# Two weight matrices cast to bf16 by the DMA that loads them, in place of f32 loads and eight cast instructions

## The chip, the core and the metric

The kernel runs on one core of one Trainium2 chip. The core has five engines with queues of their own: TensorE (PE, matmuls), VectorE (DVE), ScalarE (ACT), GpSimd (POOL) and SyncE (SP), which here issues the DMAs. Each engine takes its instructions in program order. Sixteen DMA engines move the data. The metric is the device time of one execution in microseconds (us). Five runs of the kernel before gave a median of 202.45 us (201.94 to 202.56).

## The reference

First a gated linear attention over 4 batches of 8 heads, 768 steps and head size 48: a state of 48 x 48 is scaled row by row with alpha and takes up an outer product at each step, and the output is q times the state. The heads side by side are 3072 tokens of width 384. They go through a feed-forward layer with the gate h cos(h).

```python
for t in range(S):
    state = alpha[:, :, t, :, None] * state + np.einsum('bhd,bhe->bhde', k[:, :, t], v[:, :, t])
    y[:, :, t] = np.einsum('bhd,bhde->bhe', q[:, :, t], state)
...
h = x @ w_in          # w_in  384 x 2048, f32
g = h * np.cos(h)
return (g @ w_out)    # w_out 2048 x 384, f32
```

All inputs and the output are f32; the kernel's matmuls work on bf16.

## The kernel before

The tokens are cut into 24 chunks of 128 steps, 6 per batch. For each chunk j the kernel runs a row of units, each with a letter in the dictionary `units` (lines 380 to 402); the order of all units is written out by hand in two strings, START for the first chunks and STEPS for the rest, and `run` calls them one by one. This order is the order in every engine's queue. A unit is written as its letter and a number, as in "T2": transposes of chunk 2.

The units of the attention: `a`, `k`, `v` load alpha, k and q, and v (192 KB each, in runs of 48 f32); `l` or `i` take the logarithm of alpha on ACT (L148); `C` or `c` sum it up with matmuls (L161, L165); `E` or `d` take the exponentials on ACT (L179, L181). `o` and `O` scale k and q into the tile kqb and cast v into vpb, and prepare a decay Em: in `o` all on POOL, in `O` with q on DVE (L191 to L197). `T` transposes kqb on PE (L210) and `t` copies the result out of PSUM on DVE (L216). `A` are the scores (L233), `m` masks them on DVE (L242). `S` is the state's increment (L255), `u` adds it on DVE (L267) and scales it, on POOL for most chunks (L269). `Y` are the outputs (L310), `y` copies them out on DVE (L315). The results of T, S and Y share one PSUM buffer, tagged "g".

The units of the feed-forward layer: `F` and `G` are the two halves of the first product (L329) with w1, over the first and the last 8 of 16 blocks of w_in's columns; `f` and `g` are its cosines on ACT (L337); `p` and `q` the gates on DVE (L344). `V`/`X` and `W` are the two halves of the second product (L353) with w2; `x` and `e` take the result out of PSUM, and `e` stores it. The results of C, A, F and G share three PSUM buffers, tagged "big". `w20` is 20 matmuls on a tile of zeros (L376), which fill PE's queue: 47 of them stand before c0, the first sum of logarithms, and 32 more among the units that follow.

The weights come in four loads of 1536 KB: `z0` and `z1`, the two halves of w_in's columns (in rows of 4 KB), and `Z0` and `Z1`, the two halves of w_out's rows (in rows of 1.5 KB). SP issues them into the f32 tiles w1f and w2f (L114, L128). Each half is then cast to bf16 in two pieces, one on DVE (L121; units `1` and `3`) and one on ACT (L119; units `2` and `4`): 10 and 20, 11 and 21, 30 and 40, 31 and 41.

Of the kernel before, what the change touches and what calls it, by code (L numbers as in the profile page):

```python
# [9 lines left out]
FP = mybir.dt.float32  # L10
BF = mybir.dt.bfloat16
AF = mybir.ActivationFunctionType
# [4 lines left out]
def kernel(  # L17
# [10 lines left out]
    nc = tc.nc  # L28
    B, H, S, D = q.shape
    DM, DF = moe_w_in.shape  # L30
    C = 128
# [3 lines left out]
    NF = DF // C  # L35
# [9 lines left out]
    consts = ctx.enter_context(tc.tile_pool(name="consts", bufs=1))  # L45
# [34 lines left out]
    m2 = consts.tile([C, 2], FP, tag="m2")  # L80
# [1 line left out]
    nc.vector.memset(m2[0:64, 0:1], 1.0)  # L82
    nc.vector.memset(m2[64:128, 1:2], 1.0)

    w1f = consts.tile([C, 3, DF], FP, tag="w1f")
    w1 = consts.tile([C, 3, DF], BF, tag="w1")
    w2f = consts.tile([C, NF, DM], FP, tag="w2f")
    w2 = consts.tile([C, NF, DM], BF, tag="w2")

    a_t, q_t, k_t, v_t, cp_t, icp_t = {}, {}, {}, {}, {}, {}  # L90
# [20 lines left out]
        v_t[j] = t  # L111

    def load_w1(f0, f1):
        nc.sync.dma_start(out=w1f[:, :, f0:f1],  # L114
                          in_=moe_w_in[:, f0:f1].rearrange("(k p) f -> p k f", p=C))

    def cast(eng, dst, src):
        if eng is nc.scalar:
            eng.activation(out=dst, in_=src, func=AF.Copy)  # L119
        else:  # L120
            eng.tensor_copy(out=dst, in_=src)  # L121

    def cast_w1(half, eng, k0, k1):
        f = slice(half * (DF // 2), (half + 1) * (DF // 2))
        cast(eng, w1[:, k0:k1, f], w1f[:, k0:k1, f])

    def load_w2(f):
        nc.sync.dma_start(  # L128
            out=w2f[:, f : f + 8],
            in_=moe_w_out[f * C : (f + 8) * C, :].rearrange("(f p) n -> p f n", p=C),  # L130
        )

    def cast_w2(eng, f0, f1):
        cast(eng, w2[:, f0:f1], w2f[:, f0:f1])


    table = [None]

# [234 lines left out]
    def warmup(n):  # L373
# [5 lines left out]
    dve, act_e, pool = nc.vector, nc.scalar, nc.gpsimd  # L379
# [14 lines left out]
        "i": lambda j: ln(j, 1), "c": lambda j: cums(j, 1), "d": lambda j: exps(j, 1),  # L394
        "w": warmup,

        "1": lambda h: cast_w1(h, dve, 0, 2), "2": lambda h: cast_w1(h, act_e, 2, 3),
        "3": lambda h: cast_w2(dve, 8 * h, 8 * h + 5), "4": lambda h: cast_w2(act_e, 8 * h + 5, 8 * h + 8),

        "a": load_a, "k": load_qk, "v": load_v,  # L400
        "z": lambda h: load_w1(h * (DF // 2), (h + 1) * (DF // 2)), "Z": lambda h: load_w2(8 * h),
    }

    def run(order):
# [3 lines left out]
                units[u[0]](n)  # L408

    START = (  # L410
# [6 lines left out]
    )  # L417
# [38 lines left out]
```

## Time and profile before

| | us |
|---|---|
| median of 5 runs | 202.45 |
| the profiled execution, its own time | 202.56 |
| its span | 200.8 |
| PE busy in the span | 191.1 |
| DVE / ACT / POOL busy | 126.3 / 126.5 / 78.9 |
| weight loads issued by SP at | 9.74, 21.12, 22.16, 25.49 |
| a half of w1, issue to landing | 7.6 and 8.4 |
| a half of w2, issue to landing | 11.7 and 14.0 |
| casts on DVE start at | 17.62, 30.31, 36.13, 43.02 |
| casts on ACT start at | 19.88, 29.94, 36.75, 43.44 |

A line of a timeline gives start, length, engine, line of the code, operation, output and inputs, and in brackets the idle time before it with what ended it. The chain of waits is the chain of work that ended last, followed back from the last instruction. The profiler names the tiles w1 and w2 "w", and many others "t"; lines that differ only in the buffer are told apart by their place in the hand-written order.

### The profile page before, as it was taken

Reading aid. Unit: us, or ns where it says so; the run is one execution under the profiler, and the core shown is the slowest. Engines: PE = TensorE matmul, PEld = TensorE weight load, DVE = VectorE, ACT = ScalarE, POOL = GpSimd, SP = SyncE. Lnnn points to the kernel's source line nnn. Section 1 sums busy time; section 2 is a strip of 40 time slices with the busy share of each in tenths; the row PEclk is TensorE's granted clock in tenths of the full one; section 3 lists DMA queues with packets and bytes.
Section 4 is the critical chain, followed back from the end, with each engine's and each line's share of the span. In section 5 each row is a group of like instructions: output and inputs, shape, how many; then the busy total and the mean of one; then the engine's idle time right before and its main releaser. Section 6 shows DMA issues by size and latency. Waiting matters only on the chain.

```text
span 200.8 us, 5940 instructions
## 1 busy us (share of the span) xinstructions
PE 191.1 (95%) x2535; PEld 141.1 (70%) x2535; DVE 126.3 (63%) x146; ACT 126.5 (63%) x139; POOL 78.9 (39%) x124
## 2 busy tenths in 40 slices
PE   7998979999899999999999999999999999999981
PEld 2443558597677878878877878788778778787750
DVE  6207577986966775676658656756767486658220
ACT  2024858889699379588496694795785955343510
POOL 3005190255558621923818208419471167011000
PEclk9999999999999999999999999999999999999999
DMA  6999999999898699889899799995999897100111
GB/s 121 192 285 254 218 367 340 274 173 199 167 239 170 148 183 172 173 159 185 198 188 197 160 189 163 212 194 149 205 147 131 135 185 147 42 32 12 39 58 63
DMA packets 123098, 34.47 MB, mean 172 GB/s; under 512 B 117184, under 2 KB 122304, under 8 KB 123072
## 3 DMA queue, kind: packets, MB, share of 16 engines
q1 hardware_dynamic: 123072, 34.09, 87.0%
q8 instruction: 20, 0.33, 0.7%
q14 instruction: 6, 0.05, 0.1%
HBM read 25.17 MB, written 4.72 MB: 149 GB/s over the span
## 4 chain that ended last, share of the span: by engine, by line
PE 82%; DVE 7%; issue 5%; DMA 2%; SPq 1%; POOL 1%; ACT 0%; POOLq 0%; DVEq 0%; ACTq 0%
PE t L329 31%; PE o_new L353 31%; PE t L310 7%; PE t L233 3%; DMA t<-in_k_dram 2%; DVE g_new L344 2%; PE t L210 2%; PE cum_new L161 2%; PE w_ps L376 2%; PE t L255 2%; DVE t L242 1%; DVE t L216 1%; DVE t L315 1%; SPq L105 1%; PE cum_new L165 1%
## 5 line engine op out<-in xcount | busy, mean ns | idle before, releaser
L337 ACT ACTIVATE c_sb<-t,halfpi 128x1024 bf16<-128x1024 f32 x48 | 53.4, 1115 | 33.6 <-PE t L329 33.3
L329 PE MATMUL t<-t,w 128*128 128x128 bf16 x1152 | 72.0, 219 | 1.0 <-DVE t L315 0.7
L329 PEld LDWEIGHTS <-w 128*128 128x128 bf16 x1152 | 67.0, 98 | 6.2 <-DVE t L315 0.8
L353 PE MATMUL o_new<-w,g_new 128*128 128x384 bf16 x384 | 69.9, 326 | 0.7 <-ACT o_sb L369 0.6
L344 DVE TENSOR_TENSOR g_new<-t,c_sb 128x1024 bf16<-128x1024 f32 x48 | 58.3, 1217 | 7.0 <-ACT c_sb L337 6.6
L353 PEld LDWEIGHTS <-g_new 128*128 128x128 bf16 x384 | 34.7, 98 | 22.6 <-issue 1.2
L242 DVE TENSOR_TENSOR t<-t,mask_f 128x1024 bf16<-128x1024 f32 x24 | 29.3, 1223 | 32.3 <-PE t L233 32.3
L269 POOL TENSOR_TENSOR ub<-sc,Em 128x384 bf16<-128x384 f32 x20 | 16.6, 829 | 61.9 <-DVE sc L267 61.9
L191 POOL TENSOR_TENSOR kqb<-t,icp_new 128x384 bf16<-128x384 f32 x24 | 24.8, 1034 | 27.2 <-ACT icp_new L179 19.4
L193 POOL TENSOR_TENSOR kqb<-t,cp_new 128x384 bf16<-128x384 f32 x22 | 21.9, 998 | 1.0 <-DMA t<-in_q_dram 0.9
L376 PE MATMUL w_ps<-warm 128*128 128x512 bf16 x79 | 20.9, 414 | 1.3 <-DVE warm L58 1.2
L369 ACT ACTIVATE o_sb<-o_new 128x384 f32<-128x384 f32 x22 | 10.9, 493 | 17.8 <-PE o_new L353 17.8
L315 DVE CAST t<-t 128x384 bf16<-128x384 f32 x24 | 13.4, 556 | 10.0 <-PE t L310 10.0
L195 POOL CAST vpb<-t 128x384 bf16<-128x384 f32 x24 | 12.4, 517 | 13.7 <-DMA t<-in_v_dram 12.0
L179 ACT ACTIVATE icp_new<-cum_new 128x768 f32<-128x768 f32 (+1 forms) x13 | 9.9, 762 | 9.8 <-PE cum_new L165 9.8
L141 ACT ACT_TABLE_LOAD x12 | 15.4, 1283 | 0.9 <-PEq L440 0.7
L310 PE MATMUL t<-t,vpb 128*64 128x128 bf16 x288 | 15.6, 220 | 0.4 <-DVE sc L267 0.3
L376 PEld LDWEIGHTS <-warm 128*128 128x128 bf16 x79 | 7.8, 105 | 11.2 <-issue 3.7
L148 ACT ACTIVATE lnab<-a_new 128x768 bf16<-128x768 f32 (+1 forms) x13 | 10.2, 798 | 8.5 <-DMA a_new<-in_alpha_dram 8.5
L337 ACT ACT_TABLE_LOAD x12 | 15.4, 1283 | 0.2
L310 PE MATMUL t<-t,ub 128*64 128x128 bf16 x160 | 12.9, 225 | 0.9 <-DVE t L216 0.8
L310 PEld LDWEIGHTS <-ub 128*64 128x64 bf16 x160 | 9.8, 109 | 5.4 <-issue 2.9
(43 smaller groups left out, 124.8 us busy)
## 6 DMA issues: line engine op xcount, KB each, us to landing
t<-in_v_dram SPq DMA_DIRECT2D x24, 192.0 KB, 3.9
a_new<-in_alpha_dram SPq DMA_DIRECT2D x24, 192.0 KB, 4.6
t<-in_k_dram SPq DMA_DIRECT2D x24, 192.0 KB, 4.4
t<-in_q_dram SPq DMA_DIRECT2D x24, 192.0 KB, 4.6
out_dram<-o_sb SPq DMA_DIRECT2D x24, 192.0 KB, 2.4
w1f<-in_moe_w_in_dram SPq DMA_DIRECT2D x2, 1536.0 KB, 8.0
w2f<-in_moe_w_out_dram SPq DMA_DIRECT2D x2, 1536.0 KB, 12.9
t<-kqb SPq DMA_TRANSPOSE x16, 4.3
```

Of the source, the lines that this page charges most:

```text
L141: nc.scalar.preload_act_table_set("natural_log_exp_and_others")
L191: nc.gpsimd.tensor_tensor(out=kqb[:, j % 3, 0, :, 0:D], in0=k_sb, in1=icp.rearrange("s (h d) -> s h d", h=H), op=ALU.mult)
L193: qeng.tensor_tensor(out=kqb[:, j % 3, 1, :, 0:D], in0=q_sb, in1=cp[:, 0:HD].rearrange("s (h d) -> s h d", h=H), op=ALU.mult)
L242: nc.vector.tensor_tensor(out=t.rearrange("s (h t) -> s h t", h=H), in0=A_ps.pop(j).rearrange("s (h t) -> s h t", h=H), in1=mask_f.unsquee ...
L269: eng.tensor_tensor(out=ub[:, j % 3, :, 0:96].rearrange("r p (a e) -> r p a e", a=2), in0=sc.rearrange("r p (a e) -> r p a e", a=2), in1=E ...
L310: nc.tensor.matmul(t[64 * half : 64 * half + 64, kt * C : (kt + 1) * C], lhsT, rhs, start=start, stop=stop, skip_group_check=True)
L315: nc.vector.tensor_copy(out=t.rearrange("r k t -> r (k t)"), in_=y_ps.pop(j)[:, 0 : 3 * C])
L329: nc.tensor.matmul(t[:, f], w1[:, kk, ft * C : (ft + 1) * C], x_t[j][:, kk], start=(kk == 0), stop=(kk == 2))
L337: nc.scalar.activation(out=c_sb, in_=h_ps[j, half], func=AF.Sin, bias=halfpi, scale=1.0)
L344: nc.vector.tensor_tensor(out=g_t[j][:, half * HF : (half + 1) * HF], in0=h_ps.pop((j, half)), in1=c_t.pop((j, half)), op=ALU.mult)
L353: nc.tensor.matmul(o_ps[j][:, 0:DM], g_t[j][:, ft], w2[:, ft], start=(f == 0 and (half == 0 or not whole)), stop=(f == HF - 1 and (half == ...
L376: nc.tensor.matmul(w_ps, warm[:, 0:C], warm, start=True, stop=True)
```

## The change

The f32 tiles and the eight cast instructions go. The four weight loads write bf16 straight into w1 and w2, and are issued by POOL in place of SP. In START they are placed earlier: z0 right after the first two logarithms, ahead of the warm-up matmuls; z1 after O0; Z0 after O1; Z1 after o2. On POOL's own queue z0 therefore follows the last of its constant tiles, z1 stands between O0 and O1, Z0 between O1 and u1, and Z1 between o2 and o3.

```diff
-    w1f = consts.tile([C, 3, DF], FP, tag="w1f")
     w1 = consts.tile([C, 3, DF], BF, tag="w1")
-    w2f = consts.tile([C, NF, DM], FP, tag="w2f")
     w2 = consts.tile([C, NF, DM], BF, tag="w2")
...
     def load_w1(f0, f1):
-        nc.sync.dma_start(out=w1f[:, :, f0:f1],
+        nc.gpsimd.dma_start(out=w1[:, :, f0:f1],
                           in_=moe_w_in[:, f0:f1].rearrange("(k p) f -> p k f", p=C))
-    def cast(eng, dst, src):
...
-    def cast_w1(half, eng, k0, k1):
...
     def load_w2(f):
-        nc.sync.dma_start(
-            out=w2f[:, f : f + 8],
+        nc.gpsimd.dma_start(
+            out=w2[:, f : f + 8],
             in_=moe_w_out[f * C : (f + 8) * C, :].rearrange("(f p) n -> p f n", p=C),
         )
-    def cast_w2(eng, f0, f1):
...
-        "1": lambda h: cast_w1(h, dve, 0, 2), "2": lambda h: cast_w1(h, act_e, 2, 3),
-        "3": lambda h: cast_w2(dve, 8 * h, 8 * h + 5), "4": lambda h: cast_w2(act_e, 8 * h + 5, 8 * h + 8),
...
     START = (
-        "v0 a0 k2 k0 a1 i1 a2 a4 a3 i0 w20 w20 w7 c0 d0 O0 w7 T0 z0 t0 S0 k1 10 c1 d1 l1 u0 v1 "
-        "w8 C1 O1 A0 m0 v2 w5 T1 t1 20 w6 S1 u1 A1 a5 Y0 y0 E1 o2 F0 k3 z1 Z0 v3 m1 l2 Z1 f0 v5 "
-        "T2 t2 p0 a8 Y1 y1 k4 v4 o3 a9 11 w3 S2 u2 A2 m2 N0 a6 21 F1 G0 T3 t3 f1 G1 g0 a7 Y2 k5 "
-        "p1 g1 30 C2 40 q0 y2 w3 X1 q1 A3 m3 a10 E2 S3 k6 F2 x1 f2 u3 v7 Y3 41 y3 31 G2 G3 g3 "
+        "v0 a0 k2 k0 a1 i1 a2 a4 a3 i0 z0 w20 w20 w7 c0 d0 O0 z1 w7 T0 t0 S0 k1 c1 d1 l1 u0 v1 "
+        "w8 C1 O1 Z0 A0 m0 v2 w5 T1 t1 w6 S1 u1 A1 a5 Y0 y0 E1 o2 Z1 F0 k3 v3 m1 l2 f0 v5 "
+        "T2 t2 p0 a8 Y1 y1 k4 v4 o3 a9 w3 S2 u2 A2 m2 N0 a6 F1 G0 T3 t3 f1 G1 g0 a7 Y2 k5 "
+        "p1 g1 C2 q0 y2 w3 X1 q1 A3 m3 a10 E2 S3 k6 F2 x1 f2 u3 v7 Y3 y3 G2 G3 g3 "
         "p2 k7 o4 q3 a11 X0 F3 g2 q2 T4 x0 v6 o5 W0 t4 f3 l4 A4 S4 e0 u4 N2 m4 W1 l3 p3 Y4 y4 "
```

More of the change, by code (lines that the diff above doesn't have):

```diff
@@ L113, in load_w1 @@
     def load_w1(f0, f1):
-        nc.sync.dma_start(out=w1f[:, :, f0:f1],
+        nc.gpsimd.dma_start(out=w1[:, :, f0:f1],
                           in_=moe_w_in[:, f0:f1].rearrange("(k p) f -> p k f", p=C))
-    def cast(eng, dst, src):
[L118 to L121, printed above, removed]
-    def cast_w1(half, eng, k0, k1):
-        f = slice(half * (DF // 2), (half + 1) * (DF // 2))
-        cast(eng, w1[:, k0:k1, f], w1f[:, k0:k1, f])
     def load_w2(f):
-        nc.sync.dma_start(
-            out=w2f[:, f : f + 8],
+        nc.gpsimd.dma_start(
+            out=w2[:, f : f + 8],
             in_=moe_w_out[f * C : (f + 8) * C, :].rearrange("(f p) n -> p f n", p=C),
         )
-    def cast_w2(eng, f0, f1):
-        cast(eng, w2[:, f0:f1], w2f[:, f0:f1])
     table = [None]
```

## The prediction

> **What bounds the kernel now.** I read first the busy table and the slices of the page, then the windows by stage, then the chain of waits in order of time, and last the timelines of the engines that the change touches.
>
> ```profile
> PE 191.1 (95%) x2535; PEld 141.1 (70%) x2535; DVE 126.3 (63%) x146; ACT 126.5 (63%) x139; POOL 78.9 (39%) x124
> ...
> DMA  6999999999898699889899799995999897100111
> ```
> ```profile
> 20.00:30.00 10.00, 8.24 (x117) 5.77 (x115) 6.43 (x9) 6.93 (x8) 5.79 (x9) 1.00 1.14 290
> ...
> 80.00:100.00 20.00, 20.00 (x304) 16.00 (x302) 13.47 (x15) 12.93 (x15) 12.36 (x19) 1.00 0.95 179
> ```
>
> In the windows the columns after the length are busy PE, PEld, DVE, ACT and POOL, then granted clock, DMA share and GB/s. From 60 us on PE is busy 20.00 of 20.00 us at clock 1.00: nothing that the change touches lives there, so the second 140 us pass unchanged and the start is passed on whole. All eight casts lie before 45 us. The second thing to see is the DMA row: the 16 DMA engines are full from 2 us on, so whatever is loaded earlier makes something else later.
>
> The chain of waits in the only place where a cast is on it:
>
> ```profile
> 35.13 1.00 issue
> 36.13 0.79 DVE w L121
> 36.91 0.39 issue
> 37.30 1.21 DVE g_new L344
> 38.51 0.47 DVE t L315
> 38.98 0.86 DVE g_new L344
> 40.03 1.21 DVE t L242
> 41.24 0.47 DVE sc L267
> 41.75 0.75 PE t L310 x20
> ```
>
> DVE runs gate p1 in the first "issue" (from 35.00), then cast 30 (L121), and from there it sets the pace up to Y3 at 41.75.
>
> The front of the kernel, from the timelines of ACT, PE and POOL:
>
> ```profile
> 10.21 0.94 ACT L148 ACTIVATE lnab<-a_new 128x384 bf16<-128x384 f32 x2 [8.19 <-DMA a_new<-in_alpha_dram]
> ```
> ```profile
> 14.10 0.33 PE L161 MATMUL cum_new<-lnab,triu_bf 128*128 128x384 bf16 x1
> ...
> 27.31 0.76 PE L210 MATMUL t<-ident_bf,kqb 128*128 128x128 bf16 x8
> ```
> ```profile
> 20.47 0.50 POOL L195 CAST vpb<-t 128x384 bf16<-128x384 f32 x1 [0.52 <-DMA t<-in_v_dram]
> 20.93 0.20 POOL L197 TENSOR_TENSOR Em<-cp_new,m 128x8 f32<-128x8 f32 x1
> 24.87 0.83 POOL L269 TENSOR_TENSOR ub<-sc,Em 128x384 bf16<-128x384 f32 x1 [3.74 <-DVE sc L267]
> 25.66 1.00 POOL L191 TENSOR_TENSOR kqb<-t,icp_new 128x384 bf16<-128x384 f32 x1
> 26.62 0.99 POOL L193 TENSOR_TENSOR kqb<-t,cp_new 128x384 bf16<-128x384 f32 x1
> ```
>
> The logarithms wait for alpha tile 1 (landing 10.21) and end at 11.15. The matmul c0 that reads them starts only at 14.10, when the 47 warm-up matmuls queued before it are over: alpha has 2.95 us of slack. T2 on PE (from 27.31) needs kqb of chunk 2, ready on POOL at 26.62 + 0.99 = 27.61: no slack at all.
>
> **The change part by part.** The sum is made against the profiled execution: span 200.8, time 202.56, 1.76 around the span, which I keep; it is 0.11 above the median of 202.45, so I add the difference to the median. A measurement of this kernel tells no less than about 0.2% (0.4 us) from no change.
>
> *Casts removed.* Four on DVE (1.22, 1.22, 1.25, 1.15) and four on ACT (1.06, 1.06, 1.16, 1.15). Those of w1 are hidden: the first DVE one (17.62) ends before its queue next waits for q (0.17 us on DMA), the second (30.31) is followed by a state and a mask whose readers run at 35.6, and ACT waits for PE after both of its own. The last two, 43.02 and 43.44, are followed by waits for PE or ACT (DVE 1.18 at 46.47, ACT 0.73 at 45.33). Only cast 30 at 36.13 is on the chain. Without it gate q0 runs 36.13 to 37.30, y2 and q1 end near 38.9; then m3 needs the scores A3 (PE 39.10 to 39.43, behind X1, which starts after fillers at 37.66 anyway), so m3 starts at 39.45 instead of 40.03. F2, which waited 0.38 for q1, starts at 39.77. The next late thing is A3: the gain is not 1.13 but 40.03 - 39.45 = **-0.6 us**, and PE carries it on through G2, G3, X0, F3, W0 without a gap. Bounds 0 and -1.1.
>
> *First load of w1 moved to the start, on POOL's queue.* It was issued by SP at 9.74, behind all ten first loads; now POOL issues it after its last mask instruction at 2.03 + 0.29 = 2.3, with no wait. Its 1536 KB moved at about 410 GB/s while alone (13.6 to 17.6 us), that is 3.84 us of all 16 engines. The engines are full with the 192-byte runs of q, k, v and alpha, so if the whole half goes first, alpha 1 lands at 10.21 + 3.84 = 14.05, the two logarithms end at 15.0 and c0 starts 0.9 late: **+0.9 us**, straight into the chain, since the later fillers are a fixed count. Lower bound 0: if the cast load costs by the bytes that it writes, 1.92 us, it fits in the slack of 2.95. Upper bound: at the 187 GB/s that the 192-byte runs get, 8.4 us, which is 5.4 past the slack. I take the rate of the same bytes in 4 KB rows, the nearest row. F0 at 25.96 has its weights in all these cases.
>
> The page DMA: Bandwidth & Descriptors of the Trainium skill, section Queues, rings and completion order, says that each DMA engine turns round-robin between queue rows, packet by packet; no stretch of this trace has two data queues, so it is not shown here. By it the weights would not wait behind the ten loads, as on one queue, but cut in among them. The same page's fit for loads issued by GpSimd (section Anatomy of one DMA, about 2.0 us plus bytes at 436 GB/s) gives 5.6 us for this half, an estimate; landed by 8, all of it would be ahead of alpha 1.
>
> *The other three loads on POOL.* Each issue now stands between compute on POOL. No POOL row shows such an issue; SP took 1.00 for a half of w1, and 0.49 and 4.62 for a half of w2 (the latter held up by a full queue), about 0.5 to 1.1 for the many 192 KB loads with the same 1,024 runs. I take 1.1 and keep 0.49 and 4.62 as ends.
> z1, behind O0 (end 17.05), has 1.9 us before O1 starts at 18.95, and T1 (22.06) leaves 2 us more: hidden up to 3.9.
> Z0 stands behind O1, whose v cast waits for v1, and in front of u1 (24.87) and o2, which have no slack. v1's landing, 20.47 before, has the same bytes ahead of it plus z1 if that goes first: between 20.5 and 24.3. I take the late end, as for alpha. Then the v cast and Em end at 25.0, Z0's issue at 26.1, where u1 would want 24.74 + 0.9 = 25.64: T2 is late by **+0.5 us**, and with it t2, the gate p0 behind it on DVE, and Y1, which shares the PSUM buffer. Bounds 0 (v1 early) and 25.0 + 4.62 - 25.64 = 4.0.
> Z1 behind o2 delays o3 (end 30.14), which T3 wants at 33.9: hidden up to 3.7. Landings: z1 is wanted by G0 at about 32.5, Z0 by X1 at 37.7, Z1 by W0 at 48.2; with 8.4 us, the slower landing of a half of w1, they come by about 27, 35 and 38: hidden.
>
> *SP's queue* loses four issues (7.1 us together) and runs its loads earlier; after 8 us no load is on the chain, so this is worth nothing.
>
> The sum: -0.6 + 0.9 + 0.5 = +0.8 us, 202.45 + 0.8 = **203.25**.
>
> A rule against the change, in SBUF — State Buffer of the skill (section A bandwidth-pool intuition that's wrong): DVE copies of f32 within SBUF lock GpSimd out while it writes descriptors. The DVE casts that would do so (128x2048 in 1.22 us) are the ones that leave, so by it the sum stays; no run shows it.
>
> **The rivals.**
> 1. *Everything is hidden* (the other side: faster). The place is c0, the price 0.9. If alpha 1 lands before 13.15, the point from which c0 is not delayed, and v1 early, only -0.6 is left: 201.85. For it: 2.95 us of slack, and half the bytes written. Against: DMA share 1.05 to 1.45 from 2 to 12 us, no free engine. Chance 0.22.
> 2. *Only the front is paid*: v1 comes early or the issue is short, +0.9 - 0.6 = +0.3: 202.75, no difference. Chance 0.15.
> 3. *POOL is held by its issues.* At SP's longest, 4.62, o2 is 4.0 late: -0.6 + 0.9 + 4.0 = +4.3, 206.75. For it: 1,024 runs per half of w2, and POOL idle for only 3.74 before u1. Against: SP's 4.62 was a full queue. Chance 0.15.
> 4. *The casting transfer is slow*, 8.4 us a half: c0 5.4 late, -0.6 + 5.4 = +4.8, 207.25, and more if v1 waits for a second such half (8.4 + 4.6 on 20.4 is 33.4, where S1 would want 23.8 + 5.4 = 29.2: +4.2, 211.4). For it: no cast load is in this trace. Against: nothing but the plain load's 410 GB/s. Chance 0.15.
> The forecast itself, +0.4 to +2, has 0.33.
>
> **How the numbers follow.** Slower 0.33 + 0.15 + 0.15 = 0.63, same 0.15, faster 0.22. The range reaches from the hidden case, with 0.1 for scatter, 201.75, to the case of long issues, 206.8; outside are most of rival 4 and the far ends of the others, under 2 in 10. The forecast's own range is 202.85 to 204.5.
>
> **What would show it.** Right: the logarithms start near 14 instead of 10.21, c0 near 15.0; on POOL u1 follows the issue of Z0 without idle time and T2 waits for kqb; no cast between p1 and q0, and m3 waits for A3; from 60 us on PE is full and only shifted. Wrong: c0 still at 14.10 (hidden), c0 near 19.5 (slow cast), a gap of several us on POOL before u1 (long issue), or a wait of F0, G0 or X1 for a weight, which I hold to be covered. The code could also spend time on POOL before its first issue; the sooner alpha then lands, the smaller the front term.

## The result, and the profile after

The changed kernel took a median of 203.76 us (29 runs, 202.89 to 208.08) against 202.54 us for the kernel before (53 runs, 201.61 to 204.13). The ratio is 1.0059, with a 95% interval of 1.0044 to 1.0074: slower by about 1.2 us. Medians and ranges, here and below, are of all runs; the ratios leave out runs that lie more than 1.5% above the fastest of their kernel, three of these 29. The profiled execution took 203.63 us with a span of 201.9; before it was 202.56 with 200.8. So 1.1 us of span are to be found.

The page of the changed kernel, its busy times, its DMA row, the queue that POOL feeds, and its weight loads:

```profile
PE 191.0 (95%) x2535; PEld 141.1 (70%) x2535; DVE 122.4 (61%) x142; ACT 122.5 (61%) x135; POOL 81.5 (40%) x128
...
DMA  6999999999999389889999699988994996201112
...
q0 software_dynamic: 2880, 3.15, 9.4%
...
w<-in_moe_w_in_dram POOLq DMA_DIRECT2D x2, 768.0 KB, 8.8
w<-in_moe_w_out_dram POOLq DMA_DIRECT2D x2, 768.0 KB, 10.1
```

DVE and ACT each lost four instructions and about 4 us of work, and the span grew: the work that went was not what set the end. The four loads now have a queue of their own (q0), which before did not exist, and deliver 768 KB of bf16 each, in 8.8 us (w1) and 10.1 us (w2), medians of two loads. The windows by stage, with the same columns as before the change:

```profile
20.00:30.00 10.00, 8.39 (x100) 5.57 (x99) 5.90 (x8) 5.24 (x8) 6.57 (x10) 1.00 1.20 198
80.00:100.00 20.00, 20.00 (x297) 15.78 (x295) 13.41 (x15) 13.65 (x16) 11.37 (x17) 1.00 1.03 167
```

As before, PE is full from 60 us on; every matmul there comes a constant 1.74 us later than before (57.62 became 59.36, 185.53 became 187.28). The whole difference at PE is made in the first 45 us. The chain of waits in that stretch of the changed kernel:

```profile
20.13 7.41 DMA t<-in_q_dram
...
27.61 0.84 ACT lnab L132
28.46 0.02 issue
28.48 1.28 ACT L321
29.76 0.01 issue
29.77 1.12 ACT c_sb L321
30.89 0.02 issue
30.92 1.22 DVE g_new L328
32.14 0.48 DVE t L299
32.62 0.05 issue
32.66 0.34 PE t L239 x4
...
43.50 0.75 PE t L294 x20
```

Two things are new. Cast 30 between two gates is gone from it. And a DMA stands on it at 20 us: the logarithm of unit l2, then the table load for the cosine, the cosine f0, gate p0, the copy y1 and S2 (32.66) follow one another with no gap. The profile puts the wait down to a load of q; the logarithm reads alpha of chunks 4 and 5, and it is the alpha load of chunk 5 (a5) that came last, as this answer on the DMA issues from 18.0 to 18.8 us of the changed kernel shows (KB each, then us to landing):

```profile
w<-in_moe_w_in_dram POOLq DMA_DIRECT2D x1, 768.0 KB, 9.0
a_new<-in_alpha_dram SPq DMA_DIRECT2D x1, 192.0 KB, 9.5
```

a5 was issued at 17.98 and landed at 27.5. Before, it was issued at 17.95, took 4.6 us, and l2 ran at 22.63:

```profile
22.63 0.84 ACT L148 ACTIVATE lnab<-a_new 128x768 bf16<-128x768 f32 x1 [0.29 <-DMA a_new<-in_alpha_dram]
```

S2 on the chain of the kernel before:

```profile
30.45 0.34 PE t L255 x4
```

The front, on ACT's timeline of the changed kernel:

```profile
14.48 0.94 ACT L132 ACTIVATE lnab<-a_new 128x384 bf16<-128x384 f32 x2 [12.47 <-DMA a_new<-in_alpha_dram]
...
27.61 0.84 ACT L132 ACTIVATE lnab<-a_new 128x768 bf16<-128x768 f32 x1 [3.98 <-DMA t<-in_q_dram]
```

The logarithms began at 14.48 in place of 10.21, and the matmul c0 at 15.47 in place of 14.10, with 1.15 us of idle time ahead of it that ACT ends:

```profile
15.47 0.32 PE L145 MATMUL cum_new<-lnab,triu_bf 128*128 128x384 bf16 x1 [1.15 <-ACT lnab L132]
```

POOL around the issue of Z0 (the middle line):

```profile
18.37 0.81 POOL L112 DMA_DIRECT2D w<-in_moe_w_in_dram  x1
...
22.23 0.94 POOL L116 DMA_DIRECT2D w<-in_moe_w_out_dram  x1
...
26.26 0.82 POOL L253 TENSOR_TENSOR ub<-sc,Em 128x384 bf16<-128x384 f32 x1 [3.09 <-DVE sc L251]
```

POOL stands idle for 3.09 us after that issue and u1 waits for DVE, not for POOL.

The 1.1 us are this sum of the two profiled executions (us; the first row is the first exponential on ACT, which follows c0; a positive difference is later):

| stretch | before | after | difference |
|---|---|---|---|
| start to first exponential | 14.54 | 15.91 | +1.37 |
| first exponential to S2 | 15.91 | 16.75 | +0.84 |
| S2 to Y3 | 11.30 | 10.84 | -0.46 |
| Y3 to the start of ACT's last eviction | 155.09 | 155.08 | 0 |
| that start to the end of the span | 3.96 | 3.32 | -0.64 |
| span | 200.8 | 201.9 | +1.1 |

### The profile page after: what moved, and what is told of

It reads as the page before. It is cut to its first block, busy times and chain, and to the rows that moved or that the text cites. A ratio compares the mean times of both kernels' runs of the same rounds, so it can differ in the third digit from the quotient of the medians.

```text
span 201.9 us, 5935 instructions
## 1 busy us (share of the span) xinstructions
PE 191.0 (95%) x2535; PEld 141.1 (70%) x2535; DVE 122.4 (61%) x142; ACT 122.5 (61%) x135; POOL 81.5 (40%) x128
## 4 chain that ended last, share of the span: by engine, by line
PE 79%; SPq 9%; DMA 4%; DVE 3%; ACT 2%; issue 1%; ACTq 0%; DVEq 0%
PE o_new L337 32%; PE t L313 31%; PE t L294 7%; SPq L103 6%; DMA t<-in_q_dram 4%; PE t L217 3%; SPq L98 3%; PE cum_new L145 2%; PE t L239 2%; PE t L194 1%; DVE g_new L328 1%; SPq L108 1%; DVE t L226 1%; PE cum_new L149 1%; ACT L321 1%
## 5 line engine op out<-in xcount | busy, mean ns | idle before, releaser
L175 POOL TENSOR_TENSOR kqb<-t,icp_new 128x384 bf16<-128x384 f32 x24 | 23.9, 998 | 26.3 <-ACT icp_new L163 20.2
## 6 DMA issues: line engine op xcount, KB each, us to landing
w<-in_moe_w_out_dram POOLq DMA_DIRECT2D x2, 768.0 KB, 10.1
```

Source lines behind the costliest of these rows:

```text
L175: nc.gpsimd.tensor_tensor(out=kqb[:, j % 3, 0, :, 0:D], in0=k_sb, in1=icp.rearrange("s (h d) -> s h d", h=H), op=ALU.mult)
```

## The experiments

The theory after the result: the second queue's packets take turns with those of the small loads, so that whichever small load meets a weight load lands late; casting as such costs nothing in the transfer; removed casts are worth only cast 30. The rivals: the casting makes the transfer slow, or it is GpSimd (its issues, or its way of moving data) that costs the time. In each diff below the lines of START are cut to what changes.

**1. Only the casts out.** The kernel before, without its eight casts. It leaves out what they deliver: w1 and w2 hold zeros instead, so the products of the feed-forward layer are zero.

```diff
     w2 = consts.tile([C, NF, DM], BF, tag="w2")
+    nc.vector.memset(w1, 0.0)
+    nc.vector.memset(w2, 0.0)
-  ... k1 10 c1 ... t1 20 w6 ... a9 11 w3 ... a6 21 F1 ... g1 30 C2 40 q0 ... Y3 41 y3 31 G2
+  ... k1 c1 ... t1 w6 ... a9 w3 ... a6 F1 ... g1 C2 q0 ... Y3 y3 G2
```

> The kernel before with its f32 loads where they were and only the eight casts left out (w1 and w2 are filled with zeros in DVE's idle time at the start, so the products of the feed-forward layer are zero; the amount of work is the same). The prediction's term: only cast 30 was on the chain, and the masked scores m3 then wait for A3, so 0.6 us less, about 201.9. Rival, casts off the path: no difference, 202.5. Rival, the cast's whole length counts: 1.1 less, 201.4.

Measured: 201.86 us, ratio 0.9979 [0.9961, 0.9996]. The chain of this kernel:

```profile
30.93 0.34 PE t L257 x4
...
41.77 0.75 PE t L312 x20
```

From S2 to Y3 it takes 10.84 us, exactly what the changed kernel takes, against 11.30. Removing all eight casts is worth 0.46 us, all of it in the stretch where cast 30 stands on the chain: the rest was hidden. Its whole profile came out no shorter than before's, because its warm-up matmuls ended 0.48 us later; in the ten profiles where they set it, c0 behind them starts between 13.59 and 14.58.

**2. The changed loads without the cast.** The changed placement on POOL, but f32 into w1f and w2f, with the eight casts where they had been.

```diff
-        nc.sync.dma_start(out=w1f[:, :, f0:f1],
+        nc.gpsimd.dma_start(out=w1f[:, :, f0:f1],
...
-        nc.sync.dma_start(
+        nc.gpsimd.dma_start(
             out=w2f[:, f : f + 8],
...
-  ... a3 i0 w20 ... O0 w7 T0 z0 t0 ... O1 A0 ... o2 F0 k3 z1 Z0 v3 m1 l2 Z1 f0
+  ... a3 i0 z0 w20 ... O0 z1 w7 T0 t0 ... O1 Z0 A0 ... o2 Z1 F0 k3 v3 m1 l2 f0
```

> The changed kernel's placement and issuer, but f32 loads without a cast in the DMA, and the eight casts back in their old places. If alpha is late because the 1536 KB that z0 reads take turns with it, the logarithms start at 14 to 14.5 as in the changed kernel, and with cast 30 back on the chain the time is that of the changed kernel or up to 0.6 us more, 203.8 to 204.4. If the casting in the DMA is what makes the transfer long, a plain z0 is over sooner, but all of its bytes are still ahead of alpha: then alpha lands earlier than 14.48 by what the cast costs, at least 0.5 us. If GpSimd's queue were no burden at all, c0 would be at 14.1 and the time 202.5.

Measured: 204.25 us, ratio 1.0098 [1.0073, 1.0123]. The page of this kernel:

```profile
w1f<-in_moe_w_in_dram POOLq DMA_DIRECT2D x2, 1536.0 KB, 9.0
w2f<-in_moe_w_out_dram POOLq DMA_DIRECT2D x2, 1536.0 KB, 10.4
```

The plain f32 loads landed as late as the casting ones (8.8 and 10.1), the logarithms began at 14.76, and a5 took 10.0 us. From 2 to 11 us z0 took 4.24 us of the 16 engines here (47.1% of 9 us), and 4.35 (48.3%) in the changed kernel. So the cast in the DMA costs the transfer nothing, and writing half the bytes buys nothing either. S2 to Y3 is 11.21: the price of cast 30 is back.

**3. The first weight load on another second queue.** The kernel before, with only z0 issued early, from ACT's queue.

```diff
-        nc.sync.dma_start(out=w1f[:, :, f0:f1],
+        eng = nc.scalar if f0 == 0 else nc.sync
+        eng.dma_start(out=w1f[:, :, f0:f1],
...
-  v0 a0 k2 k0 a1 i1 ... T0 z0 t0
+  v0 a0 k2 k0 a1 z0 i1 ... T0 t0
```

> The kernel before (f32 loads, all casts, the other three loads where they were); only z0 is issued early, from ACT's queue, right behind SP's first alpha loads in the code and without a wait. If a second queue is what lets the weight load cut in, whoever fills it, alpha lands near 14.5 and c0 near 15.4 as in the changed kernel, and the time is 202.5 + 1.4, about 203.9. If it is GpSimd's way of issuing, alpha lands near 10.2 as before, and the time is 202.5.

Measured: 204.10 us (203.94 to 204.16), ratio 1.0089 [1.0071, 1.0108]. ACT's timeline of this kernel:

```profile
0.73 0.49 ACTq L115 DMA_DIRECT2D w1f<-in_moe_w_in_dram  x1
...
14.77 0.94 ACT L149 ACTIVATE lnab<-a_new 128x384 bf16<-128x384 f32 x2 [12.24 <-DMA a_new<-in_alpha_dram]
```

Without GpSimd and without a cast the logarithms wait just as long, and the first exponential comes at 16.20. The front's price is that of either second queue tried here, POOL's or ACT's, that starts a large load there. What the two queues get while the weight packets run is seen in the changed kernel from 5 to 9 us, and in this kernel from 4 to 7 us (packets, MB, share of the 16 engines; q0 and q10 carry the weights, q1 the small loads):

```profile
q0 software_dynamic: 335, 0.68, 92.5%
q1 hardware_dynamic: 442, 0.08, 14.6%
```
```profile
q10 hardware_dynamic: 287, 1.18, 96.2%
q1 hardware_dynamic: 286, 0.05, 9.1%
```

The turns are nearly packet for packet, 287 to 286 here and 335 to 442 there. But a weight packet takes eight to ten times an engine's time of a small one (an estimate from these shares and counts: about 0.17 against 0.02 us), so the small loads almost stop. The page DMA: Bandwidth & Descriptors of the Trainium skill, section Queues, rings and completion order, has each DMA engine go round-robin between queue rows, a packet at a time; the counts agree with it, in the packets that the profile counts.

**4. Alpha first on SP.** The changed kernel, with the loads that the chain needs first put first on SP's queue.

```diff
-  v0 a0 k2 k0 a1 i1 a2
+  a0 a1 k0 v0 k2 i1 a2
```

> The changed kernel with SP's first loads in the order a0 a1 k0 v0 k2 in place of v0 a0 k2 k0 a1. c0 is back at 14.1 in every theory. If the late first alpha is the whole loss, the time falls by 1.4 us to about 202.3. If the alpha of chunks 4 and 5 (landing about 27.5 because z1 and Z0 take turns with it) is a second late load behind the first one, its logarithm still starts at about 27.6, the cosine f0 behind it on ACT at about 29.8, and the time stays at about 203.8, although c0 is 1.4 earlier.

Measured: 206.15 us (203.12 to 209.52), ratio 1.0136 [1.0081, 1.0191]. c0 was back at about 14.5, and yet its shortest run was no shorter than the median of the kernel before beside it (202.63). a5 now took 13.2 us to land, and PE stood still ahead of S2. The profile is that of the longest of the six runs, 209.52 us. PE's timeline of this kernel, and then its windows:

```profile
36.36 0.50 PE L239 MATMUL t<-vpb,kqb 128*128 128x96 bf16 x4 [5.54 <-DVE t L299]
```
```profile
34.00:38.00 4.00, 1.64 (x19) 1.30 (x20) 2.72 (x4) 3.15 (x3) 0.70 (x1) 0.52 1.19 210
38.00:42.00 4.00, 4.00 (x49) 4.00 (x47) 0.67 (x1) 1.16 (x2) 1.45 (x3) 0.63 0.75 145
42.00:46.00 4.00, 3.94 (x66) 3.01 (x64) 3.60 (x5) 3.31 (x3) 0.00 (x0) 1.00 1.35 195
```

The granted clock (third column from the end) is 0.52 where PE comes back from the gap, and 1.00 again from 41 us on. Here a late load is paid for twice: by the wait, and by the slow matmuls behind it. The page TensorE: Matmul & The Clock Gate, section Part 1: The HAM clock gate, gives the gate a free-running window of about 3.4 us. An estimate from that, which no run here tests: a gap near that length would trip it in some executions and not in others. The scatter would agree, as the six runs had mean clocks from 0.983 to 1.000. In the profiles a gap of 3.30 us, a little under the page's window, was followed by a clock of 0.50 (experiment 5); gaps of 2.1 us, in experiments 3 and 7, were not.

The same instructions ran once more: the function that runs the order takes no unit number from 24 up, so the fillers w27, put ahead of S2, fell out.

```diff
-  a9 w3 S2
+  a9 w3 w27 S2
```

> The kernel with alpha first (z1 and Z0 as in the changed kernel) with 27 filler matmuls more ahead of S2, 5.8 us at full clock, which covers the idle time of 5.5 us. If the clock falls because PE stood idle, it stays at 1.00 and the time is what the late alpha alone leaves, 203.5 to 205. If it falls for another reason, 207 or more.

Measured: 204.91 us (203.23 to 209.44), ratio 1.0104 [1.0064, 1.0143]. In the profiled execution, which kept clock 1.00 and took 203.53 us, v1 was caught as well as a5, as POOL's timeline shows:

```profile
24.57 0.50 POOL L179 CAST vpb<-t 128x384 bf16<-128x384 f32 x1 [4.62 <-DMA t<-in_v_dram]
```

a5 landed there after 9.0 us, and S2 came at 32.46, as in the changed kernel (32.66). Even at full clock, alpha first gains nothing while z1 stands where it does.

**5. a5 early too.** Experiment 4 with a5 moved in front of i0.

```diff
-  v0 a0 k2 k0 a1 i1 a2 a4 a3 i0 ... A1 a5 Y0
+  a0 a1 k0 v0 k2 i1 a2 a3 a4 a5 i0 ... A1 Y0
```

> As the kernel with alpha first, and the alpha of chunk 5 loaded right behind that of chunk 4, ahead of z1. If the two late loads of alpha are the whole loss, both are gone and the gain of the casts is left: 202.5 - 0.5, about 202.0. If POOL's issues or the other transfers cost something by themselves, it stays above 202.5.

Measured: 206.94 us, ratio 1.0230 [1.0189, 1.0272]; a miss by 5 us. POOL's timeline and the windows of this kernel:

```profile
26.70 0.50 POOL L179 CAST vpb<-t 128x384 bf16<-128x384 f32 x1 [6.02 <-DMA t<-in_v_dram]
```
```profile
24.00:26.00 2.00, 0.00 (x0) 0.00 (x0) 0.00 (x0) 0.29 (x1) 0.00 (x0) 1.00 1.22 231
26.00:28.00 2.00, 0.74 (x12) 0.60 (x11) 0.23 (x1) 0.00 (x0) 1.30 (x3) 0.59 0.72 134
28.00:32.00 4.00, 3.15 (x38) 2.80 (x35) 2.02 (x3) 0.00 (x0) 3.77 (x7) 0.50 1.08 167
```

With a5 out of the way, z1 catches the next load, v1 (issued 17.20, landed 9.45 us later; Z0 was issued only at 27.31, so z1 alone did this). S1 waits for it, 3.30 us on PE, and the clock falls to 0.50. Saving one load moves the loss to another: the cause is z1's place, not a5's.

**6. Fillers across the gap.** Experiment 4 with 12, and then with 27 filler matmuls more ahead of S2, to see whether the idle gap is what lowers the clock.

```diff
-  a9 w3 S2
+  a9 w3 w12 S2
```

> The kernel with alpha first (and z1, Z0, Z1 as in the changed kernel), with 12 filler matmuls more ahead of S2, where PE stood idle for 4.6 us in the profile and the granted clock then fell to 0.50 for some 6 us. If that fall of the clock is the effect of the idle time, and costs 2 to 3 us, the clock stays at 1.00 and the time falls from 206.2 to about 203.5. If the clock falls for another reason (its work, its heat), the time stays at 206 or rises by the fillers' 2.6.

Measured: 208.42 us, ratio 1.0179 [1.0129, 1.0228]. a5 came still later (13.8 us), PE stood still for 3.91 us in spite of the fillers, and the clock fell again: no answer.

```diff
-  a9 w3 S2
+  a9 w3 w20 w7 S2
```

> The kernel with alpha first (z1 and Z0 as in the changed kernel), with 27 filler matmuls more ahead of S2, now as two units of 20 and 7 (the run before this one left its 27 out: the order's loop takes numbers below 24 only, so it was the kernel with alpha first once more). They hold S2 back to 36.4 in any case, where it started at 32.5 with the alpha landing at 27.4, so 203.3 + 3.9, about 207.2. What tells the theories apart is the clock: if it falls because PE stands idle, it stays at 1.00 in all runs, and the times lie close together; if it falls for another reason, some runs have 0.98 to 0.99 again, and up to 3 us more than the others.

Measured: 208.30 us (207.24 to 211.56), ratio 1.0270 [1.0234, 1.0305]. PE's timeline of this kernel:

```profile
29.56 6.86 PE L360 MATMUL w_ps<-warm 128*128 128x512 bf16 x29 [0.16 <-issue]
36.25 0.33 PE L239 MATMUL t<-vpb,kqb 128*128 128x96 bf16 x4
```

Kept busy, PE goes into S2 at full clock (0.33 us for its four matmuls against 0.50 in experiment 4), and five of six runs show 0.997 or more. The sixth (211.56 us) shows 0.991, so idle time as the cause of the low clock is supported and not settled.

**7. The weights later.** z1 behind O1, Z0 behind o2, Z1 behind o3, so that each meets other small loads; once with alpha first, once with the old order on SP.

```diff
-  v0 a0 k2 k0 a1 i1 ... O0 z1 w7 ... O1 Z0 A0 ... o2 Z1 F0 ... o3 a9
+  a0 a1 k0 v0 k2 i1 ... O0 w7 ... O1 z1 A0 ... o2 Z0 F0 ... o3 Z1 a9
```

> The changed kernel with alpha first on SP, and z1, Z0, Z1 each one place later on POOL (z1 behind O1, Z0 behind o2, Z1 behind o3). If the loss comes from small loads that are caught by a weight load and land some 9 us after their issue, then the alpha of chunks 4 and 5 (issued at 18) is down before z1 starts at 21, f0 is at 27.5 again and the gain of the casts is left: 202.6 - 0.5, about 202.1; Z0, due at 37.7 and landing about 38.5, may take back up to 0.8. If casting or issuing on POOL costs by itself, it stays above 203.

Measured: 201.52 us (201.03 to 202.50), ratio 0.9955 [0.9938, 0.9972]. This is below both kernels. ACT's timeline, and the chain, of this kernel:

```profile
22.69 0.84 ACT L132 ACTIVATE lnab<-a_new 128x768 bf16<-128x768 f32 x1 [0.78 <-DMA a_new<-in_alpha_dram]
```
```profile
30.13 0.34 PE t L239 x4
...
40.96 0.75 PE t L294 x20
```

a5 lands in 4.6 us again, the logarithm of l2 runs at 22.69 as before the change (22.63), S2 comes at 30.13 (30.45 before) and Y3 10.83 later. Both losses are gone. In the profiles the span is 1.5 us shorter than before: 0.35 at the front, which the warm-up matmuls set here and which moves by as much on its own, 0.47 by the casts and 0.70 at the end of the program.

```diff
-  O0 z1 w7 ... O1 Z0 A0 ... o2 Z1 F0 ... o3 a9
+  O0 w7 ... O1 z1 A0 ... o2 Z0 F0 ... o3 Z1 a9
```

> The same three loads later, with SP's old order of the first loads. If the late first alpha and the late second alpha are two separate terms, the second is gone and the first stays: c0 at 15.4, 202.6 + 1.4 - 0.5, about 203.5. If only the later one of the two counts, it is as fast as the kernel with alpha first, about 202.1.

Measured: 202.85 us (202.55 to 203.16), ratio 1.0022 [1.0008, 1.0036]. Here the logarithms begin at 14.51, as in the changed kernel; a5 lands in 4.7 us; the first exponential to S2 takes 15.95. That is the front's price alone, +1.39, with the casts (-0.47) and the shorter end (-0.65): +0.27 in the profiles, whose spans are 201.1 and 200.8. The expectation was too high by the shorter end, which it did not hold.

**8. What the cast in the DMA is worth where a weight is late.** Experiment 7 with alpha first, but with f32 loads and the eight casts: experiment 2's kernel in this order.

```diff
-  v0 a0 k2 k0 a1 i1 ... O0 z1 w7 ... O1 Z0 A0 ... o2 Z1 F0 ... o3 a9
+  a0 a1 k0 v0 k2 i1 ... O0 w7 ... O1 z1 A0 ... o2 Z0 F0 ... o3 Z1 a9
```

> The fastest kernel so far (alpha first, z1, Z0, Z1 one place later on POOL), with f32 loads and the eight casts back in their old places. If the DMA's cast is worth what cast 30 costs on the chain and no more, it is slower than that kernel by 0.5 to 0.6 us, about 202.0 to 202.1. If casting in the DMA itself speeds the loads up or slows them down, the difference is larger, or nothing.

Measured: 203.11 us (201.33 to 204.37), ratio 1.0027 [1.0001, 1.0053]; 1.6 above experiment 7's first kernel. PE's timeline of this kernel:

```profile
38.71 1.47 PE L352 MATMUL o_new<-w,g_new 128*128 128x384 bf16 x8 [1.25 <-DVE w L127]
```

Z0 lands at about 37.5, its casts follow, and X1 waits 1.25 us for them. In experiment 7's first kernel Z0 lands at about 36.8 and is bf16 already on landing, and X1 starts at 37.39 without a wait. So in an order with late weights the casting load removed more than cast 30: it took a cast out of the path of the weight, which also came some 0.65 us earlier.

**9. Cast 30 on POOL.** The kernel before, with cast 30 moved from DVE to POOL, between kqb and vpb of chunk 3.

```diff
+        if j == 3:
+            cast_w2(nc.gpsimd, 0, 5)
         nc.gpsimd.tensor_copy(out=vpb[:, j % 3, :, 0:D], in_=v_sb)
-  g1 30 C2
+  g1 C2
```

> The kernel before, all loads as they were; only cast 30 goes from DVE to POOL, between the k and q products and the v cast of chunk 3, where POOL stands idle from 30.1 to 34.9. At POOL's 0.5 us for 384 elements it takes 2.5 us, from Z0's landing near 33.9 to 36.4, in time for X1 at 37.7. If cast 30 is the only one on the chain, this gains what all eight gain, 0.5 to 0.6 us: about 202.1. If X1 or the v cast then waits for POOL, nothing or a loss.

Measured: 202.50 us, ratio 0.9999 [0.9981, 1.0018]. POOL's timeline of this kernel:

```profile
36.45 1.78 POOL L121 CAST w<-w2f 128x1920 bf16<-128x1920 f32 x1 [6.73 <-DMA w2f<-in_moe_w_out_dram]
```

The half of w2 landed only at 36.45, the cast took 1.78 us and X1 waited for it, 1.04 us. SP had issued this load at 23.84, against 22.16 before, so the profile shows why this execution gained nothing; that it holds for the other runs is likely by their median, and not shown.

## Why the prediction was right, and where its steps were not

The forecast was 203.25 us, slower; measured were 203.76. The total is nearer than its terms deserve: one term was nothing, one was too small and two were missing, and that they nearly cancel is luck.

*Casts, -0.6 predicted, -0.46 measured.* The mechanism held: all of the gain lies between S2 and Y3, where only cast 30 stands on the chain (experiment 1 removes all eight), and the next late thing is A3, for which the mask m3 waits 0.60 us in the changed kernel. The mask began 9.10 us after S2, not 9.00, and 9.58 before.

*The first load at the front, +0.9 predicted, +1.37 measured.* Right in its place and its path: the logarithms wait for alpha, and the slack of the warm-up matmuls is used up. The mis-sized term is the delay of alpha, taken as 3.84 us of engine time at the rate of a lone load; it was 4.27 (10.21 to 14.48), and 4.55 and 4.56 in experiments 2 and 3. Beside the small loads the weights were dearer: 4.35 us of all 16 engines. They went nearly as a whole ahead of alpha 1, as the step had it, and landed at 11.0. But alpha 1 was not in flight with them. SP's queue of the changed kernel, and then of the kernel before:

```profile
5.92 4.13 SPq L103 DMA_DIRECT2D t<-in_q_dram  x1
10.09 4.05 SPq L98 DMA_DIRECT2D a_new<-in_alpha_dram  x4
```
```profile
4.66 0.75 SPq L105 DMA_DIRECT2D t<-in_q_dram  x1
5.45 4.25 SPq L100 DMA_DIRECT2D a_new<-in_alpha_dram  x4
```

The issue of q of chunk 0 took 4.13 us in place of 0.75 while the weights ran, so alpha 1, the first of the four, was issued at 10.09 in place of 5.45; from its issue to the logarithms it then took no longer than before. Of the +1.37, about half a us is uncertain, since c0 in the kernel before is set by the warm-up matmuls, which move by that much.

*Z0's issue, +0.5 predicted, nothing measured.* The issue took 0.94 us (1.1 was taken). But v1 landed early, issued at 16.17 and there 4.2 us later, so Z0's issue was over at 23.2 and u1 waited for DVE. The step had v1 behind the whole of z1; z1 was issued only at 18.37.

*The rest of POOL and the weights.* No matmul waited for a weight, as held. The issues took 0.81 to 0.94 us each, also in experiment 2, where the DVE casts of f32 stayed. Only one of those casts overlapped an issue there, by 0.2 us, so whether a cast on DVE holds up an issue on POOL is not shown. A product on POOL beside a cast was slower: in the kernel before the one at 43.21, beside cast 31, took 1.82 us, and the same operation at 25.66 took 1.00; neither the cast nor this product is on the chain.

*The step that failed* is the sentence on SP's queue: "after 8 us no load is on the chain, so this is worth nothing". It holds for the kernel before, where a5 landed with its wait hidden. In the changed kernel z1, with Z0 behind it, catches a5, which lands 4.9 us later, and the chain through l2, the table load, f0, p0 and y1 makes S2 0.84 us later. The price of the second queue was charged to the load at 2 us and to v1, and not to the others that are in flight while z1 runs. Experiment 7 shows it: with z1, Z0 and Z1 later, this 0.84 is gone (15.95 and 15.94 against 15.91 before). What z1 and Z0 each add to a5's delay was not separated.

*A term that the prediction did not have*, -0.64 at the end. From ACT's last eviction to the end of the span, 3.91 to 4.02 us pass in the four profiles of kernels where SP issues three or four of the weight loads (before, and experiments 1, 3 and 9), and 3.24 to 3.33 in the ten where POOL issues all four, with casts or without. The last stretch holds two packets of queue q14, which the profile lists as one for instructions, in those four, and one in the ten. SP's program has four DMA issues fewer; that this saves a load of code at its end is a guess, which no experiment tried.

So 0.84 stood in for the 0.5 that did not happen, the front was 0.5 dearer, and the end paid for it. Of the rivals, the one in which only the front is paid had its conditions met, a short issue and an early v1, but the loss by a5 took the place of the other. A slow casting transfer is refuted by experiment 2, and that POOL is held by its issues is refuted by their 0.94 us. That everything is hidden would have needed alpha in time, and experiment 7 shows that ordering can bring it about.

## What to carry to other kernels

A load moved to a second queue no longer waits its turn: while its packets ran they had over nine tenths of the DMA engines' time here (92.5% and 96.2%), from POOL's queue or ACT's, with a cast or without. So list every small load that is in flight or still to be issued while it runs, and follow each to its first reader. Mending one victim moves the loss to the next; move the large load to where nothing urgent is in flight, and put the loads that the chain needs first at the head of their queue. A removed instruction pays only up to the next late thing (0.46 us of eight casts here), and a cast in the DMA is worth most where the weight itself is late.

## What had not been expected of the hardware

- Two queues took turns nearly packet for packet (287 to 286 in experiment 3), so the one with the weight rows had 96.2% of the engines' time and the one with 192-byte runs 9.1%.
- A load that casts f32 to bf16 landed as fast as the plain f32 one from the same queue: 8.8 against 9.0 us for w1, 10.1 against 10.4 for w2.
- Gaps on PE of 3.3 and 5.5 us were followed by about 7 us at a granted clock of 0.50 (experiments 4 and 5), and the kernel of experiment 4 scatters over 6.4 us, while the first kernel of experiment 7 stays within 1.5 us.
- The end of the program became 0.65 us shorter with the weight loads off SP's queue; its cause stays open.
